# A linear-attention and SwiGLU kernel: w as token pairs, output weights four rows per partition, two sums moved from TensorE to VectorE, and another order

## The chip, the cores and the metric

The kernel runs on one core of one Trainium2 chip. The metric is the device time of one execution in microseconds (us). TensorE is called PE in the profile, its weight loads PEld, VectorE DVE, ScalarE ACT, GpSimd POOL and SyncE SP.

## What is computed

A linear attention with decay (batch 4, 8 heads, 768 tokens, 48 channels per head) feeds an RMS norm and a SwiGLU feed-forward layer (FFN) over 3072 tokens of width 384, with 1536 hidden units.

```python
for t in range(S):                                   # r, k, v, w: [4, 8, 768, 48]
    cur = einsum('bhd,bhe->bhde', u[None] * k[:, :, t], v[:, :, t])
    y[:, :, t] = einsum('bhd,bhde->bhe', r[:, :, t], state + cur)
    state = w[:, :, t, :, None] * state + einsum('bhd,bhe->bhde', k[:, :, t], v[:, :, t])
x = y.transpose(0, 2, 1, 3).reshape(3072, 384)
xn = x / sqrt(mean(x * x, -1) + 1e-6) * rms_g
g = xn @ w_gate
out = (g * sigmoid(g) * (xn @ w_val)) @ w_out
```

Inputs and the output are float32 in HBM; the matmuls take bf16.

## The kernel before, in words

The 768 tokens are cut into six superblocks n = 0 to 5 of 128 tokens; each has four batches j = 0 to 3. A block (n, j) is 128 tokens on the partitions by 8 heads x 48 channels. The recurrence inside a block becomes matmuls: with the sums of log w over the tokens, r and k are scaled by exponentials of these sums, their products are masked to the past, and a state per head carries what earlier blocks left. When the four blocks of a superblock are through, its 512 normalized tokens go through the FFN as 12 hidden groups f of 128 units.

Every piece of work is a small function of (n, j) or (n, f), and the string ORDER calls them one by one. The scheduling is by hand: each engine executes its instructions in just that order, and each DMA queue issues in it too. The steps that matter here, with their lines:

- load_w, load_k, load_r, load_v (L221, L208): 192 KB each, on SP's queue, 128 partitions x 8 heads x 192 bytes. Eight buffers of each kind; at most eight of SP's DMAs are under way, since each waits for the one eight places before it.
- ln (L195 through the helper act): the logarithm of w on ScalarE. cs_mm (L370, L373, L375): on TensorE the sums of log w before each token (mask_lt, into ps_a), the whole block's decay as four one-column products, and minus the sums from each token on (mask_nle, into ps_b).
- exp_r, exp_k (ScalarE), r_mul, k_mul (VectorE, L397, L402): the scaled r and k, as bf16 in rk. In superblock 1 the exponentials go to SBUF tiles er and ek.
- rk_pe and rk_tr: r and k transposed, in superblocks 0 and 1 by TensorE (L425) and a ScalarE copy (L434), later by DMA transposes on SP's queue (L430).
- q_mm (L443, L445), q_mask_e, q_copy_o, q_mask_o: the products of r and k, masked. y_mm (L488, L491): the block's output. st_mm (L468, L471) and st_new (L479): the new state, which is the old one (L468, a matmul with the identity) plus k times v, times the decay.
- bonus_mul (L408, L409), bonus_sum (L413), bonus_v (L418): the u term, mostly on GpSimd.
- x_add (L496), x_sq, x_rstd, xn_mul, then xn_pe and xn_out or, in superblocks 4 and 5, xn_tr (a DMA transpose) and xn_gain: the normalized tokens, transposed, as xnt.
- gate_mm and val_mm (L546), silu, h_mul (L564), o_mm (L606), o_out, out_dma: the FFN. ps_a and ps_b have two banks each, so gate_mm of group f waits for silu of f-2, and val_mm for h_mul of f-2.
- load_gv (L306) and load_wo (L312): the FFN's weights, on GpSimd's own queue, cast to bf16 on the way. load_gv.0 brings hidden groups 0 to 3, load_gv.1 groups 4 to 11; the last figure is 0 for the gate, 1 for the value. The first of each pair waits until load_w.1.0 has landed; load_wo waits for load_v.1.1. All stand among GpSimd's other steps and are issued in its turn.

Of the kernel before, what the change touches and what calls it, by code (L numbers as in the profile page):

```python
# [9 lines left out]
FP32 = mybir.dt.float32  # L10
BF16 = mybir.dt.bfloat16
AF = mybir.ActivationFunctionType
ALU = mybir.AluOpType

LN_EXP = "natural_log_exp_and_others"
# [10 lines left out]
load_w.0.0 load_v.0.0 load_w.0.1 load_k.0.0 load_r.0.0 ln.0.0 load_w.0.2 load_r.0.1 ln.0.1 cs_mm.0.0 load_k.0.1  # L26
cs_mm.0.1 exp_k.0.0 load_w.0.3 exp_r.0.0 k_mul.0.0 bonus_mul.0.0 exp_r.0.1 r_mul.0.0 load_r.0.2 exp_k.0.1 w_tot.0.0
cast_v.0.0 rk_pe.0.0 load_k.0.2 ln.0.2 r_mul.0.1 st_mm.0.0 rk_tr.0.0 cs_mm.0.2 load_w.1.0 st_new.0.0 bonus_mul.0.1
load_v.0.1 q_mm.0.0 k_mul.0.1 ln.0.3 w_tot.0.1 bonus_sum.0.0 rk_pe.0.1 load_k.0.3 exp_k.0.2 q_mask_e.0.0 exp_r.0.2
cs_mm.0.3 bonus_v.0.0 q_mask_o.0.0 rk_tr.0.1 load_r.0.3 k_mul.0.2 y_mm.0.0 bonus_mul.0.2 exp_k.0.3 load_w.1.1  # L30
r_mul.0.2 q_mm.0.1 exp_r.0.3 x_add.0.0 ln.1.0 rk_pe.0.2 load_v.0.2 bonus_sum.0.1 x_sq.0.0 q_mask_e.0.1 cast_v.0.1
load_v.0.3 bonus_v.0.1 w_tot.0.2 rk_tr.0.2 q_mask_o.0.1 cs_mm.1.0 load_w.1.2 k_mul.0.3 bonus_mul.0.3 q_mm.0.2
bonus_sum.0.2 load_k.1.0 r_mul.0.3 ln.1.1 q_mask_o.0.2 rk_pe.0.3 load_w.1.3 x_rstd.0.0 cast_v.0.2 y_mm.0.1 bonus_v.0.2
load_r.1.0 rk_tr.0.3 x_add.0.1 load_gv.0.0 load_r.1.1 q_mask_e.0.2 cast_v.0.3 xn_mul.0.0 load_gv.0.1 bonus_sum.0.3
q_mm.0.3 ln.1.2 bonus_v.0.3 y_mm.0.2 x_sq.0.1 q_mask_e.0.3 st_mm.0.1 exp_k.1.0 load_gv.1.1 w_tot.0.3 x_add.0.2
x_rstd.0.1 cs_mm.1.1 q_mask_o.0.3 exp_r.1.0 load_gv.1.0 x_sq.0.2 y_mm.0.3 exp_k.1.1 load_v.1.0 xn_pe.0.0 x_rstd.0.2
x_add.0.3 st_mm.0.2 st_new.0.1 xn_mul.0.1 x_sq.0.3 st_new.0.2 st_mm.0.3 cs_mm.1.2 x_rstd.0.3 xn_out.0.0 xn_mul.0.2
# [12 lines left out]
load_r.2.0 cs_mm.2.0 q_copy_o.1.3 h_mul.0.11 y_mm.1.2 x_sq.1.0 load_w.2.2 st_mm.1.2 x_add.1.1 o_mm.0.0 st_new.1.2  # L50
x_rstd.1.0 x_sq.1.1 load_r.2.1 exp_k.2.0 x_rstd.1.1 ln.2.1 load_k.2.1 k_mul.2.0 exp_r.2.0 q_mask_o.1.3 bonus_sum.1.3
o_mm.0.1 cast_v.1.3 load_r.2.2 o_out.0.0 xn_mul.1.0 bonus_v.1.3 w_tot.2.0 x_add.1.2 load_v.2.0 bonus_mul.2.0 x_sq.1.2
y_mm.1.3 load_v.2.1 o_out.0.1 st_mm.1.3 x_add.1.3 ln.2.2 cs_mm.2.1 load_w.2.3 st_new.1.3 o_mm.0.2 x_sq.1.3 x_rstd.1.2
exp_k.2.1 r_mul.2.0 load_k.2.2 xn_mul.1.1 x_rstd.1.3 k_mul.2.1 xn_mul.1.2 bonus_sum.2.0 out_dma.0.0 cs_mm.2.2
exp_r.2.1 cast_v.2.0 o_out.0.2 xn_pe.1.0 xn_pe.1.1 load_r.2.3 r_mul.2.1 bonus_mul.2.1 xn_pe.1.2 xn_mul.1.3 o_mm.0.3
xn_out.1.0 exp_r.2.2 load_k.2.3 xn_out.1.1 ln.2.3 rk_tr.2.0 xn_out.1.2 exp_k.2.2 w_tot.2.1 r_mul.2.2 cast_v.2.1
xn_pe.1.3 cs_mm.2.3 o_out.0.3 bonus_mul.2.2 xn_out.1.3 st_mm.2.0 load_v.2.2 exp_r.2.3 w_tot.2.2 st_mm.2.1 k_mul.2.2
load_k.3.0 exp_k.2.3 gate_mm.1.0 r_mul.2.3 w_tot.2.3 val_mm.1.0 load_r.3.0 silu.1.0 k_mul.2.3 bonus_mul.2.3
gate_mm.1.1 bonus_sum.2.1 rk_tr.2.1 val_mm.1.1 q_mm.2.0 silu.1.1 h_mul.1.0 gate_mm.1.2 load_r.3.1 bonus_v.2.0
h_mul.1.1 load_k.3.1 val_mm.1.2 silu.1.2 q_mask_e.2.0 gate_mm.1.3 h_mul.1.2 rk_tr.2.2 bonus_mul.3.0 val_mm.1.3  # L60
silu.1.3 st_new.2.0 gate_mm.1.4 q_copy_o.2.0 rk_tr.2.3 bonus_sum.2.2 val_mm.1.4 h_mul.1.3 silu.1.4 cast_v.2.2
# [596 lines left out]
```

## Time and profile before

| | us |
|---|---|
| median of 5 runs | 213.05 (212.78 to 213.16) |
| the profiled execution | 212.78 |
| its span (first to last instruction) | 210.8 |
| first FFN matmul starts | 29.67 |
| first o_mm starts | 56.27 |
| first FFN matmul of superblock 5 starts | 175.74 |
| last matmul ends | 207.54 |
| HBM read / written | 25.96 MB / 4.72 MB |

The profile's page gives each engine's busy time and share of the span, and a line of digits per engine: the span in 40 equal slices of 5.3 us, each digit the busy tenths of a slice (9 is 90% or more). Groups of instructions are named by line, engine, operation and tiles (output, an arrow, inputs). A timeline line reads: start, duration, engine, line, operation, tiles, shape, count, and in brackets the idle time before it and what ended that. A line of stretches reads: from:to, length, then for PE, PEld, DVE, ACT and POOL the busy time and the number of instructions, then TensorE's granted clock, the DMA engines' mean busy share and GB/s. A DMA queue's line reads: packets, MB, and the packets' time as a share of 16 engines. A matmul's own duration holds its latency, which overlaps the next; the spacing of starts is its price.

### The profile page before, as it was taken

The page shows a single profiled execution, that of the slowest core. Times are in us where ns is not written, and L with a number is a line of the kernel's source. Part 1 is how long each engine was busy: PE and PEld are TensorE (multiplying, and loading weights), DVE is VectorE, ACT ScalarE, POOL GpSimd, SP SyncE. Part 2 cuts the span into 40 slices and gives each one's busy share as a digit, 9 for nine tenths or more (in the row PEclk, how much of TensorE's full clock was granted, in tenths as well). Part 3 has the DMA queues.
Part 4 walks back from the last instruction along what each step waited for, and adds up shares of the span by engine and source line. Part 5 has one row for each costly group of instructions (what it writes and reads, how often), then busy time and mean ns, then how long its engine had stood idle before and what let it go on. Part 6 is the DMA issues. An engine that isn't in the chain of part 4 may idle for free.

```text
span 210.8 us, 4399 instructions
## 1 busy us (share of the span) xinstructions
PE 195.1 (93%) x1552; PEld 107.4 (51%) x1552; DVE 148.5 (70%) x295; ACT 138.4 (66%) x282; POOL 109.2 (52%) x167
## 2 busy tenths in 40 slices
PE   5676879799899999999999999999999999999993
PEld 2454533454566445665454665455655544544563
DVE  6498852899979778988689699767876755235411
ACT  3786995567988556987546998578858873225300
POOL 3498500698699593798697789573222520000000
PEclk9999999999999999999999999999999999999999
DMA  6999999999999999999999999981187030000122
GB/s 128 210 201 177 170 201 201 210 182 210 173 192 236 167 185 226 210 210 192 211 192 208 197 249 171 227 181 44 54 190 124 20 84 13 37 0 37 40 112 76
DMA packets 126878, 32.41 MB, mean 154 GB/s; under 512 B 120580, under 2 KB 126088, under 8 KB 126856
## 3 DMA queue, kind: packets, MB, share of 16 engines
q1 hardware_dynamic: 123664, 28.58, 67.3%
q0 software_dynamic: 3184, 3.54, 10.2%
q8 instruction: 12, 0.20, 0.4%
q14 instruction: 10, 0.08, 0.1%
q10 hardware_dynamic: 8, 0.00, 0.0%
HBM read 25.96 MB, written 4.72 MB: 146 GB/s over the span
## 4 chain that ended last, share of the span: by engine, by line
PE 72%; DMA 10%; SPq 9%; DVE 4%; issue 2%; ACT 1%; ACTq 0%
PE ps_q L606 22%; PE ps_a L546 19%; PE ps_b L546 19%; DMA rt<-in_r_dram 8%; SPq L208 6%; SPq L221 3%; PE ps_q L443 2%; DMA rkT<-rk 2%; PE ps_q L491 2%; PE ps_q L488 2%; PE ps_b L375 1%; DVE ht L564 1%; PE ps_a L370 1%; DVE rk L397 1%; PE ps_q L468 1%
## 5 line engine op out<-in xcount | busy, mean ns | idle before, releaser
L564 DVE TENSOR_TENSOR ht<-ps_b,sg 128x512 bf16<-128x512 f32 x72 | 48.6, 688 | 25.1 <-PE ps_b L546 17.6
L195 ACT ACTIVATE sg<-ps_a 128x512 bf16<-128x512 f32 x72 | 42.7, 596 | 35.0 <-PE ps_a L546 34.7
L546 PE MATMUL ps_b<-xnt,wv_sb 128*128 128x512 bf16 x216 | 59.1, 382 | 0.8 <-DVE ht L564 0.7
L546 PE MATMUL ps_a<-xnt,wg_sb 128*128 128x512 bf16 x216 | 59.7, 386 | 0.0
L606 PE MATMUL ps_q<-wo_sb,ht 128*128 128x384 bf16 (+1 forms) x300 | 49.9, 319 | 0.0
L408 POOL TENSOR_TENSOR ruk<-rt,kt 128x384 f32<-128x384 f32 x24 | 24.3, 1012 | 24.8 <-DMA rt<-in_r_dram 21.3
L606 PEld LDWEIGHTS <-ht 128*128 128x128 bf16 x300 | 28.4, 98 | 16.8
L546 PEld LDWEIGHTS <-wg_sb 128*128 128x128 bf16 x216 | 20.2, 99 | 23.3 <-issue 1.5
L546 PEld LDWEIGHTS <-wv_sb 128*128 128x128 bf16 x216 | 20.1, 98 | 23.2 <-issue 2.7
L409 POOL TENSOR_TENSOR ruk<-ruk,u_bc 128x384 f32<-128x384 f32 x24 | 24.6, 1023 | 1.9
L418 POOL TENSOR_TENSOR ydiag<-vt,diag 128x384 f32<-128x384 f32 x24 | 19.8, 831 | 3.1 <-DVE diag L413 2.9
L461 POOL TENSOR_SCALAR_AFFINE_SELECT qts<-qts 128x512 bf16<-128x512 bf16 x20 | 12.7, 637 | 14.3 <-ACT qts L454 14.3
L450 DVE TENSOR_TENSOR qts<-ps_q,mask_lt 128x512 bf16<-128x512 f32 x24 | 16.2, 684 | 4.0 <-issue 2.5
L496 DVE TENSOR_TENSOR xb<-ps_q,ydiag 128x384 f32<-128x384 f32 x24 | 13.2, 552 | 5.3 <-PE ps_q L491 4.8
L195 ACT ACTIVATE lw<-wt 128x384 bf16<-128x384 f32 x24 | 12.0, 515 | 5.2 <-DMA wt<-in_w_dram 5.1
L501 ACT ACTIVATE junk<-xb 128x384 bf16<-128x384 f32 x24 | 12.4, 518 | 3.9 <-DVE xb L496 3.8
L514 ACT ACTIVATE xn<-xb,rstd 128x384 bf16<-128x384 f32 x24 | 14.4, 606 | 0.9 <-POOL rstd L510 0.6
L454 ACT CAST qts<-ps_q 128x512 bf16<-128x512 f32 x20 | 11.6, 584 | 4.7 <-PE ps_q L445 4.7
L193 ACT ACT_TABLE_LOAD x10 | 12.8, 1283 | 1.8 <-PEq L642 1.6
L613 DVE COPY ob<-ps_q 128x384 f32<-128x384 f32 (+1 forms) x13 | 7.0, 538 | 9.1 <-PE ps_q L606 9.0
L615 ACT COPY ob<-ps_q 128x384 f32<-128x384 f32 (+1 forms) x12 | 5.6, 463 | 11.9 <-PE ps_q L606 11.9
L402 DVE TENSOR_TENSOR rk<-kt,ps_b 128x384 bf16<-128x384 f32 x20 | 11.0, 548 | 3.3 <-DMA kt<-in_k_dram 1.6
(71 smaller groups left out, 276.4 us busy)
## 6 DMA issues: line engine op xcount, KB each, us to landing
wt<-in_w_dram SPq DMA_DIRECT2D x24, 192.0 KB, 4.0
vt<-in_v_dram SPq DMA_DIRECT2D x24, 192.0 KB, 4.1
kt<-in_k_dram SPq DMA_DIRECT2D x24, 192.0 KB, 3.8
rt<-in_r_dram SPq DMA_DIRECT2D x24, 192.0 KB, 3.8
out_dram<-ob SPq DMA_DIRECT2D x23, 192.0 KB, 2.8
wo_sb<-in_moe_w_out_dram POOLq DMA_DIRECT2D x3, 384.0 KB, 7.4
wv_sb<-in_moe_w_val_dram POOLq DMA_DIRECT2D x1, 768.0 KB, 10.9
wg_sb<-in_moe_w_gate_dram POOLq DMA_DIRECT2D x1, 768.0 KB, 14.4
```

What stands on the lines that cost most here:

```text
L193: nc.scalar.preload_act_table_set(table_name)
L195: return nc.scalar.activation(**kw).ins
L408: nc.gpsimd.tensor_tensor(out=ruk[n, j], in0=inp["r", n, j], in1=inp["k", n, j], op=ALU.mult)
L409: nc.gpsimd.tensor_tensor(out=ruk[n, j], in0=ruk[n, j], in1=u_bc, op=ALU.mult)
L418: nc.gpsimd.tensor_tensor(out=ydiag[n, j], in0=inp["v", n, j], in1=diag[n, j].to_broadcast([128, H, D]), op=ALU.mult)
L450: nc.vector.tensor_tensor(out=qts[n, j][:, 0], in0=bank["q", n, j][0], in1=bc_mid(mask_lt, NP), op=ALU.mult)
L461: nc.gpsimd.affine_select(out=qts[n, j][:, 1], in_=qts[n, j][:, 1], compare_op=ALU.is_gt, fill=0.0, base=0, pattern=[[0, NP], [1, 128]], c ...
L496: nc.vector.tensor_tensor(out=xb[n, j], in0=bank.pop(("y", n, j)), in1=ydiag[n, j].rearrange("p h d -> p (h d)"), op=ALU.add)
L514: nc.scalar.activation(out=xn, in_=xb[n, j], func=AF.Copy, scale=rstd[n, j][:, 1:2])
L546: nc.tensor.matmul(ps, lhsT=ws[:, c, f * 128:(f + 1) * 128], rhs=xnt[n][:, c, :], start=(c == 0), stop=(c == KC - 1))
L564: nc.vector.tensor_tensor(out=ht[n][:, f, :], in0=bank.pop(("v", n, f)), in1=bank.pop(("sg", n, f)), op=ALU.mult)
L606: nc.tensor.matmul(ps[:, cols], lhsT=ht[n][:, f, b * L:(b + 1) * L], rhs=wo_sb[:, f, cols], start=(f == 0), stop=(f == FC - 1))
```

## The change

- W_PAIR = (0, 1): w of superblocks 0 and 1 is loaded with two neighbouring tokens per partition (384 bytes in a row), batch j even on partitions 0 to 63 and j odd on 64 to 127. One ln and one cs_mm then serve two batches; cs_pair makes the sums with 64-row matmuls (eight of 384 columns and sixteen of one column for two batches) and masks mp_lt and mp_nle, which GpSimd builds at the start, after its other constants.
- load_wo puts four consecutive rows of w_out on one partition. So hidden unit 4m + i of a group of 512 stands at partition m, and the gate and value weights are read with a step of four columns (units).
- The gate and value weights have one tile for each load (wg_sb0, wg_sb4, wv_sb0, wv_sb4).
- OLD_DVE = (2, 3, 4): the old state is added by VectorE in PSUM, not by a matmul with the identity.
- ONE_SUM = (4, 5): the sum for k is made by VectorE from the sum for r and log w (cs_add); exp_k takes it with a factor of -1, and the mask_nle matmul goes.
- ORDER is replaced by another.

```diff
-    W_PAIR = ()
+    W_PAIR = (0, 1)
     Q_PAIR = ()
-    OLD_DVE = ()
+    OLD_DVE = (2, 3, 4)
+    ONE_SUM = (4, 5)
...
-    wg_sb = persist.tile([128, KC, DF], BF16)
-    wv_sb = persist.tile([128, KC, DF], BF16)
+    wg_sb = [persist.tile([128, KC, (b - a) * 128], BF16, name="wg_sb%d" % a) for a, b in zip(GV, GV[1:])]
+    wv_sb = [persist.tile([128, KC, (b - a) * 128], BF16, name="wv_sb%d" % a) for a, b in zip(GV, GV[1:])]
...
-            in_=moe_w_out[g * FG * 128:(g + 1) * FG * 128, :].rearrange("(c p) m -> p c m", p=128)).ins
+            in_=moe_w_out[g * FG * 128:(g + 1) * FG * 128, :].rearrange("(p c) m -> p c m", c=FG)).ins
...
-        nc.tensor.matmul(b[:, 0:DM].rearrange("p (h d) -> p h d", h=H), lhsT=mask_nle, rhs=rhs,
-                         start=True, stop=True)
+        if n not in ONE_SUM:
+            nc.tensor.matmul(b[:, 0:DM].rearrange("p (h d) -> p h d", h=H), lhsT=mask_nle, rhs=rhs,
+                             start=True, stop=True)
+
+    def cs_add(n, j):
+        b = bank["cs_k", n, j] = psB.tile([128, 512], FP32, name="ps_b")
+        nc.vector.tensor_tensor(out=b[:, 0:DM].rearrange("p (h d) -> p h d", h=H),
+                                in0=bank["cs_r", n, j][:, NP:NP + DM].rearrange("p (h d) -> p h d", h=H),
+                                in1=lw[:, n % 2, j, :, 0:D], op=ALU.add)
...
+    def units(ws, c, f):
+        g = max(i for i, x in enumerate(GV) if x <= f)
+        a = (f // FG * FG - GV[g]) * 128
+        return ws[g][:, c, a:a + FG * 128].rearrange("p (m i) -> p i m", i=FG)[:, f % FG, :]
+
     def fc_mm(ps, ws, n, f):
         for c in range(KC):
-            nc.tensor.matmul(ps, lhsT=ws[:, c, f * 128:(f + 1) * 128], rhs=xnt[n][:, c, :],
+            nc.tensor.matmul(ps, lhsT=units(ws, c, f), rhs=xnt[n][:, c, :],
```

The add of the old state was in the code already, behind the switch: st_new begins with `nc.vector.tensor_tensor(out=ps, in0=ps, in1=st[:, n % 2, j], op=ALU.add)` for a superblock in OLD_DVE, and st_mm leaves its identity matmul out.

The new order up to the first FFN groups, in the parts that the prediction speaks of. SP's queue:

```text
before: w00 v00 w01 k00 r00 w02 r01 k01 w03 r02 k02 w10 v01 k03 r03 w11 v02 v03 w12 k10 w13 r10 r11 v10 k11 v11 k12 k13 r12 r13 w20 v12 ...
after:  w00 w01 k00 r00 k01 v00 r01 k02 w02 r02 w03 v01 v02 w10 r03 k03 w11 r10 k10 w12 w13 k11 r11 v03 k12 r12 v10 v11 k13 r13 v12 w20 ...
```

GpSimd's queue, from bonus_mul.0.3 on:

```text
before: bonus_mul.0.3 bonus_v.0.2 load_gv.0.0 load_gv.0.1 bonus_v.0.3 load_gv.1.1 load_gv.1.0 bonus_mul.1.0 ...
after:  bonus_mul.0.3 bonus_mul.1.0 bonus_v.0.2 load_gv.0.0 load_gv.0.1 bonus_v.0.3 load_gv.1.0 bonus_mul.1.1 load_gv.1.1 ...
```

TensorE, from xn_pe.0.2 on (cs_mm.1.3 stood here before; after, all sums of superblock 1 are done):

```text
before: xn_pe.0.2 xn_pe.0.3 cs_mm.1.3 gate_mm.0.0 val_mm.0.0 gate_mm.0.1 val_mm.0.1 gate_mm.0.2 val_mm.0.2 gate_mm.0.3 val_mm.0.3 rk_pe.1.0 gate_mm.0.4 val_mm.0.4 ...
after:  rk_pe.1.0 xn_pe.0.2 xn_pe.0.3 gate_mm.0.0 val_mm.0.0 gate_mm.0.1 rk_pe.1.1 q_mm.1.0 val_mm.0.1 gate_mm.0.2 val_mm.0.2 q_mm.1.1 gate_mm.0.3 val_mm.0.3 rk_pe.1.2 st_mm.0.1 gate_mm.0.4 val_mm.0.4 ...
```

In the rest, attention and FFN stay interleaved as before, with single steps moved by a few places. st_mm.0.1, 0.2 and 0.3 come after the first FFN groups instead of before them.

## The prediction

> **What bounds the kernel now.** I read the page's busy table first, then its slices.
>
> ```profile
> PE 195.1 (93%) x1552; PEld 107.4 (51%) x1552; DVE 148.5 (70%) x295; ACT 138.4 (66%) x282; POOL 109.2 (52%) x167
> ...
> PE   5676879799899999999999999999999999999993
> ...
> DMA  6999999999999999999999999981187030000122
> ```
>
> TensorE is full from the seventh slice on; before that it has holes, while the DMA engines are full from the second slice to the 27th. So there are two regimes. I cut the span where they meet: the first FFN matmul (29.67 us), the end of the last long wait (38.06), the first output matmul (56.27), the first FFN matmul of superblock 5 (175.74). The busy times of these stretches, in the order PE, weight loads, DVE, ACT, POOL:
>
> ```profile
> 0.00:29.67 29.67, 19.93 (x177) 12.49 (x177) 21.27 (x48) 21.99 (x51) 16.30 (x28) 1.00 0.98 180
> 29.67:38.06 8.39, 7.11 (x25) 2.68 (x24) 2.63 (x7) 4.54 (x7) 0.49 (x1) 1.00 1.14 209
> 38.06:56.27 18.21, 17.40 (x169) 9.52 (x170) 17.89 (x29) 13.87 (x22) 14.86 (x17) 1.00 1.14 200
> 56.27:175.74 119.47, 119.04 (x1007) 65.53 (x1005) 94.26 (x195) 89.08 (x187) 77.51 (x122) 1.00 0.84 168
> ```
>
> Up to 38 us the DMA sets the pace; from 38 to 56 VectorE has 17.89 of 18.21 us filled and TensorE waits for it here and there; from 56 on TensorE is never free and VectorE has 94.26/119.47 = 79%. What ends the first regime is one load, seen in the timelines of VectorE and TensorE:
>
> ```profile
> 37.44 0.56 DVE L397 TENSOR_TENSOR rk<-rt,er 128x384 bf16<-128x384 f32 x1 [2.45 <-DMA rt<-in_r_dram]
> ...
> 38.06 0.62 PE L425 MATMUL ps_q<-ident,rk 128*128 128x128 bf16 x8 [1.28 <-DVE rk L397]
> ```
>
> In the chain of waits this load (load_r.1.0) lies from 20.97 to 37.42 us, 16.4 us for a transfer that takes 3.8 at the median. The DMA view of 23 to 36 us says why:
>
> ```profile
> q0 software_dynamic: 1458, 2.18, 91.8%
> q1 hardware_dynamic: 2107, 0.40, 23.9%
> ```
>
> Weights (POOL's queue, q0) and loads (SP's, q1) share the engines roughly packet against packet. A weight packet takes 96 or 172 ns and a load's 192-byte packet 15 ns (the trace's packet records), so while weights flow SP's queue nearly stands: 2107 packets, two loads, in 13 us, against one load in 0.95 us before (17,358 packets of 1024 per load from 4 to 20 us). The weight phase ran from its first packet at 21.8 us to its last at 37.1 us, 15.3 us.
>
> **The price list of TensorE** is the spacing of starts where nothing waits:
>
> ```profile
> 55.14 0.32 PE L370 MATMUL ps_a<-lw,mask_lt 128*128 128x384 bf16 x1
> 55.31 0.24 PE L373 MATMUL ps_a<-ones_col,lw 128*128 128x1 bf16 x4
> 55.41 0.32 PE L375 MATMUL ps_b<-lw,mask_nle 128*128 128x384 bf16 x1
> 55.57 0.33 PE L488 MATMUL ps_q<-st,rkT 128*128 128x96 bf16 x4
> 55.74 0.36 PE L491 MATMUL ps_q<-vb,qts 128*128 128x48 bf16 x8
> 55.94 0.32 PE L468 MATMUL ps_q<-st,ident 128*128 128x384 bf16 x1
> 56.10 0.33 PE L471 MATMUL ps_q<-vb,rk 128*128 128x96 bf16 x4
> ```
>
> A 384-column matmul costs 0.16 us, cs_mm 0.43, y_mm 0.37, st_mm 0.33 (half of it the old state); in the same way gate_mm or val_mm is 0.65, o_mm 1.95, rk_pe 0.46, q_mm 0.33. Summed over the order, the program needs 179.3 us of TensorE.
>
> **Token pairs and the new load order.** Eight loads of w have 512 packets of 384 bytes in place of 1024 of 192. Packets of 192, 256 and 768 bytes took 15, 18 and 36 ns, so 384 bytes lies between 18 and 36, near 22 by the straight line; a load then takes 512 x 22.5 ns / 16 engines = 0.72 us in place of 0.96. But each fills only 64 partitions, which no row shows, so I keep 0 to 0.24 us saved per load (a loss is possible too, if fewer engines share it; loads queued behind would fill the others). The Trainium skill, "SBUF — State Buffer", section "Door 1: The DMA port swizzle", speaks against it: a transfer to partitions 0 to 63 reaches half of the ports and ran at 196 GB/s there. By that a pair load is 1.0 us, nothing is saved, and my sum would be about 1 us higher.
>
> SP's queue now takes r and k of batches 0 and 1 and k of batch 2 of superblock 1 ahead of the weights, and v.0.3 only as its 24th load (18th before). POOL issues the first weights after bonus_mul.1.0, which needs k.1.0, the 19th load. The first load landed at 3.76 us and the next followed 0.96 apart, so the 19th lands at 3.76 + 18 x 0.96 = 21.0, less six pair loads, 19.6 to 21.0. POOL adds bonus_mul (2.07) and bonus_v (0.83): the first weights are issued at 22.6 to 24.0 in place of 19.91, the first packet follows 1.9 later as it did before, the phase takes 14.3 to 15.3, and landing 0.5 more: **the last gate/val weights are there at 39.3 to 41.7 us, not 37.64**. I take 40.6, in the middle. The attention of superblock 0 ends near 30 us as now: v.0.3 lands at 23.9 to 25.8, and bonus_v, x_add, x_sq, x_rstd, xn_mul, xn_pe, xn_out follow with 5 us (0.83, 0.56, 0.61, 0.52, 0.60, 0.50, 0.56 and hand-overs). So val_mm.0.4, which reads the last piece, starts at 40.6 instead of 39.16: **+1.4 us** (0.1 to 2.5). Queued behind it on TensorE is the whole FFN, and behind that VectorE's h_mul.
>
> The paired cs_mm (24 matmuls for two batches, 12 before) comes wholly before the first FFN matmul. Eight 384-column products on half the rows cost 0.65 us if the two halves run side by side, 1.3 if not; q_mm's eight 128-column products on 48 rows take 0.33 us where 8 x 0.053 = 0.43 would be serial, so halves do overlap, and I take 1.05 with the 16 one-column ones. TensorE is busy 19.93 of 29.67 us there, which hides 4 x 0.2 us. The extra masks on POOL (ten instructions near 0.3 us, as its mask rows) end near 5.8 us, when the first pair of w is through its Ln: at most 0.5 us, before a start that the loads set anyway.
>
> **What TensorE has left at val_mm.0.4.** By the order: 163.9 us before, 159.4 after. The 4.5 us are: twelve old-state matmuls gone, 12 x 0.1625 = 1.95; eight mask_nle matmuls gone, 1.30; rk_pe.1.1, 1.2 and q_mm.1.0, 1.1 already done while weights were awaited, 1.58; st_mm.0.2 and 0.3 still to do, +0.34.
>
> **Stalls after it.** Before, 39.16 to 207.54 is 168.4 us for 163.9 of work: 2.1 stalled until o_mm.0.0, 2.4 after it. Until o_mm.0.0 VectorE's work falls from 16.4 to 11.9 us (r_mul and k_mul of three batches, 0.56 to 1.26 us each, are done earlier) against 13.6 of TensorE; I take 0.7, a gain of 1.4. Afterwards VectorE gets twelve adds of the old state and eight of the decay sum; x_add, which reads PSUM and SBUF likewise, takes 552 ns, so 11.0 us more, 105 of about 116: 90% instead of 79%. TensorE lost about 2 us in the 18 us where VectorE had 98%, and 2.4 in the 151 after; I take 1.5 more, nearer to the latter.
>
> **The weights' layout.** Output weights come as 128 larger packets per load instead of 512; at the straight line through 79, 96 and 172 ns for 768, 1024 and 2048 bytes a 3072-byte packet takes 250 ns, 2.0 us per load instead of 2.5, hidden at 45 to 57 us behind the FFN. They also hold SP's queue harder (24 turns per engine instead of 96); the loads behind are due at 49 us or later, and if v.1.2 misses that, it costs 1 to 2 us. Gate and val weights are now read with a step of four elements. No row has such a read: below 216 ns per weight load it costs nothing, since 0.648 us per three matmuls covers the present 98 ns; a load of 300 ns would cost 432 x 0.084 = 36 us. I take nothing, the nearest row being 98. The skill's "TensorE: Matmul & The Clock Gate", section "Weight-path perf modes — Fast Weight Load (FWL) and DoubleRow", lets the fast load take such a step, and its section "LDWEIGHTS (loading the stationary operand)" gives P/1.2, 107 ns for 128 columns, without it; only its remark on 16-byte lines in "SBUF — State Buffer" speaks of a penalty. By either the sum stays.
>
> **The sum**, against the profiled execution (212.78 us, span 210.8; the median of the runs is 213.05): +1.4 - 4.5 - 1.4 + 1.5 = -3.0, so **209.8 us**.
>
> **Rivals.** (1) *VectorE becomes the bound*, from o_mm.1 to the FFN of superblock 4. Against it: 25.2 us of VectorE lie free there and only 11 are asked for. For it: from o_mm.2.0 to gate_mm.3.0 the new order has 10.3 us of VectorE for 9.8 of TensorE, and the add stands in st_new ahead of the scaling while h_mul waits behind it, which frees the PSUM that val_mm needs. If each of three such stretches loses 2 us, as 38 to 56 did, with 1.5 already counted: 209.8 + 4.5 = 214.3, slower. It decides once the added stalls exceed 4.5 us. (2) *The weights come later still*: v.0.3 or v.1.0, now last in SP's queue, are caught behind weight packets (48 turns per engine at 187 ns); cast_v.1.0 then holds ScalarE's silu.0.5. 1 to 3 us: 211 to 212.8. (3) *The strided weight read is not hidden*: 213 to 245. (4) *The new order's stalls vanish altogether* and pairs save in full: 209.8 - 1.5 - 1.2 = 207.1.
>
> **Numbers.** Forecast with (4) 0.48, all but 0.02 of it faster; rival (2) 0.19, of it 0.12 faster, 0.04 the same, 0.03 slower; rival (1) 0.28, slower but for 0.02 faster; (3) 0.05, slower. Faster by over 0.2% (what a measurement here can tell from no change): 0.60; the same 0.06; slower 0.34. The range 206.8 to 215.2 leaves out the strided case, the worst of (1) and some luck below; the forecast's own is 207.0 to 212.0.
>
> **What would show it.** Right: wv_sb's last piece landing near 40.6, rk_pe.1.0 ahead of the first gate_mm, no wait of 1 us on r of superblock 1, TensorE's busy time down by some 2.5 us, VectorE's up to about 158, gate_mm spacing still 0.65. Wrong: waits of val_mm on h_mul between 85 and 160 us; loads of v landing beyond 45 us with silu waiting; gate_mm spacing above 0.65; paired loads as slow as plain ones.

## The result, and the profile after

The changed kernel takes 214.23 us (median of 43 runs, 213.05 to 216.54) against 213.01 us (80 runs) for the kernel before: a ratio of 1.0068 [1.0054, 1.0081], 0.7% slower where 209.8 us was forecast. Some executions of every kernel fall into a slower state; all ratios here compare executions in the faster one, while the medians of the experiments take in all of theirs. Its profiled execution took 214.61 us, span 212.9.

The busy table and two slice lines of the page after, as they were shown of before:

```profile
PE 193.6 (91%) x1580; PEld 114.5 (54%) x1580; DVE 158.2 (74%) x315; ACT 137.7 (65%) x278; POOL 112.5 (53%) x177
...
PE   3367775999999999999999899999999999999993
...
DMA  5999999999997999887999869994398031100022
```

TensorE is busy 1.5 us less (2.5 forecast) and VectorE 9.7 us more (158 forecast). But TensorE's slices are thinner at the start (3 3 6 7 against 5 6 7 6), and it is full only from the eighth slice on. The same stretches, cut at the first gate_mm, val_mm.0.4, the first o_mm and the first FFN matmul of superblock 5 (from:to, length, then PE, weight loads, DVE, ACT, POOL):

```profile
0.00:35.10 35.10, 20.18 (x221) 13.96 (x221) 23.64 (x47) 22.25 (x48) 24.04 (x42) 1.00 1.02 187
35.10:45.52 10.42, 10.42 (x63) 5.25 (x64) 4.95 (x8) 6.93 (x11) 3.88 (x5) 1.00 1.04 194
45.52:59.19 13.67, 13.50 (x118) 7.67 (x117) 12.53 (x25) 10.39 (x20) 8.33 (x13) 1.00 1.04 200
59.19:178.33 119.14, 118.14 (x1005) 69.33 (x1003) 105.47 (x219) 89.08 (x186) 76.27 (x119) 1.00 0.81 164
```

The start is 35.10 us long instead of 29.67. Behind it TensorE is never free again: val_mm.0.4 does not wait for weights, and VectorE, with 105.47 of 119.14 us (89%, forecast 90%), holds up nothing for long. From val_mm.0.4 to the last matmul (209.66) it is 164.14 us; before it was 168.38 (39.16 to 207.54). So the forecast's -4.4 for everything behind val_mm.0.4 is measured as -4.24, and the whole error lies ahead of it: val_mm.0.4 starts at 45.52 instead of 39.16, **+6.4 where +1.4 was forecast**.

In one point these rows mislead. They give a granted clock of 1.00 from the start, but the traces of the two kernels hold no clock record ahead of 33.29 us (before) and 40.52 us (after). The matmuls show a slower TensorE until then. In the changed kernel a gate_mm or val_mm takes 1.28 us (36.33 to 37.61) until about 40.4 us, and 0.65 (44.88 to 45.52) behind that; before, the change comes at 33.4 us. The last line is val_mm.0.4, which starts without a wait:

```profile
36.33 1.48 PE L561 MATMUL ps_b<-xnt,wv_sb 128*128 128x512 bf16 x3
37.61 1.48 PE L561 MATMUL ps_a<-xnt,wg_sb 128*128 128x512 bf16 x3
...
44.88 0.81 PE L561 MATMUL ps_a<-xnt,wg_sb 128*128 128x512 bf16 x3
45.52 0.81 PE L561 MATMUL ps_b<-xnt,wv_sb 128*128 128x512 bf16 x3
```

The wait for load_r.1.0, which ended the start before, is gone. In its place TensorE waits for the normalization (timeline of TensorE, changed kernel; L435 is rk_pe.1.0, L535 xn_pe, L561 the first gate_mm):

```profile
31.08 1.06 PE L435 MATMUL ps_q<-ident,rk 128*128 128x128 bf16 x8
...
33.86 0.50 PE L535 MATMUL ps_q<-ident,xn 128*128 128x128 bf16 x3 [1.39 <-ACT xn L524]
35.10 1.44 PE L561 MATMUL ps_a<-xnt,wg_sb 128*128 128x512 bf16 x3 [0.74 <-DVE xnt L546]
```

xn comes from ScalarE, so the start is read on ScalarE. Its busy time up to the first silu, first of the kernel before, then of the changed one (ACT is the fourth pair of figures):

```profile
0.00:32.03 32.03, 22.29 (x182) 13.35 (x183) 21.90 (x49) 24.15 (x54) 16.30 (x28) 1.00 0.99 181
```

```profile
0.00:37.56 37.56, 22.64 (x226) 14.81 (x227) 23.64 (x47) 24.68 (x52) 24.04 (x42) 1.00 1.03 188
```

The work is the same, 24.15 and 24.68 us; the idle time is 7.9 us before and 12.9 after. Its waits for loads up to there (total, times, longest), of before, then of the changed kernel:

```profile
ACT lw L195 <- DMA wt<-in_w_dram: 5.1, 6, 1.4
ACT vb L330 <- DMA vt<-in_v_dram: 0.6, 1, 0.6
```

```profile
ACT lw L197 <- DMA wt<-in_w_dram: 6.8, 4, 2.2
ACT vb L332 <- DMA vt<-in_v_dram: 2.9, 1, 2.9
```

In the changed kernel these are 2.2 us for the first pair of w, 2.9 for v.0.0 (cast_v.0.0 stands ahead of exp_k.0.0), 1.2, 1.5 and 1.9 for w.0.3, w.1.1 and w.1.3. The last of these, in the timeline of ScalarE:

```profile
24.42 0.84 ACT L197 ACTIVATE lw<-wt 128x768 bf16<-128x768 f32 x1 [1.91 <-DMA wt<-in_w_dram]
25.17 0.51 ACT L511 ACTIVATE junk<-xb 128x384 bf16<-128x384 f32 x1
...
31.98 0.52 ACT L511 ACTIVATE junk<-xb 128x384 bf16<-128x384 f32 x1 [0.21 <-DVE xb L506]
...
37.56 0.60 ACT L197 ACTIVATE sg<-ps_a 128x512 bf16<-128x512 f32 x1
```

ln.1.2 waits for w.1.3, and the first x_sq of superblock 0 (L511) stands behind it. From there ScalarE has 13.1 us of queue, in which the timeline shows one gap, of 0.21 us, and the first silu is its end. Before, the last wait of this kind was cast_v.0.3:

```profile
21.06 0.51 ACT L330 CAST vb<-vt 128x384 bf16<-128x384 f32 x1 [0.63 <-DMA vt<-in_v_dram]
...
29.84 0.49 ACT L195 ACTIVATE ek<-ps_b 128x384 f32<-128x384 f32 x1 [0.23 <-PE ps_b L375]
...
32.03 0.60 ACT L195 ACTIVATE sg<-ps_a 128x512 bf16<-128x512 f32 x1
```

That is 10.97 us from the wait to the silu.

### The profile page after: what moved, and what is told of

Its sections match the earlier page's. It is cut to its first block, busy times and chain, and to the rows that moved or that the text cites. A ratio compares the mean times of both kernels' runs of the same rounds, so it can differ in the third digit from the quotient of the medians.

```text
span 212.9 us, 4495 instructions
## 1 busy us (share of the span) xinstructions
PE 193.6 (91%) x1580; PEld 114.5 (54%) x1580; DVE 158.2 (74%) x315; ACT 137.7 (65%) x278; POOL 112.5 (53%) x177
## 4 chain that ended last, share of the span: by engine, by line
PE 73%; DVE 8%; SPq 7%; ACT 3%; issue 3%; DMA 2%; POOL 2%; POOLq 0%; DVEq 0%; ACTq 0%
PE ps_q L621 21%; PE ps_a L561 20%; PE ps_b L561 20%; SPq L210 4%; SPq L223 3%; DMA kt<-in_k_dram 2%; PE ps_q L453 2%; DVE ht L579 2%; PE ps_q L501 1%; PE ps_q L498 1%; DVE rk L407 1%; PE ps_q L481 1%; PE ps_a L373 1%; PE ps_q L535 1%; ACT junk L511 1%
## 5 line engine op out<-in xcount | busy, mean ns | idle before, releaser
L561 PE MATMUL ps_a<-xnt,wg_sb 128*128 128x512 bf16 x216 | 59.9, 387 | 1.0 <-DVE xnt L546 1.0
L579 DVE TENSOR_TENSOR ht<-ps_b,sg 128x512 bf16<-128x512 f32 x72 | 49.2, 687 | 14.5 <-PE ps_b L561 10.1
L561 PE MATMUL ps_b<-xnt,wv_sb 128*128 128x512 bf16 x216 | 59.3, 384 | 0.1
L561 PEld LDWEIGHTS <-wg_sb 128*128 128x128 bf16 x216 | 23.4, 115 | 21.9 <-issue 2.9
L561 PEld LDWEIGHTS <-wv_sb 128*128 128x128 bf16 x216 | 22.9, 114 | 19.3 <-issue 1.5
L471 POOL TENSOR_SCALAR_AFFINE_SELECT qts<-qts 128x512 bf16<-128x512 bf16 x20 | 13.1, 656 | 20.8 <-ACT qts L464 20.8
L423 DVE TENSOR_REDUCE diag<-ruk 128x8 f32<-128x384 f32 x24 | 12.9, 544 | 5.2 <-POOL ruk L419 5.2
L628 DVE COPY ob<-ps_q 128x384 f32<-128x384 f32 (+1 forms) x13 | 7.0, 541 | 13.1 <-PE ps_q L621 13.0
L197 ACT ACTIVATE lw<-wt 128x384 bf16<-128x384 f32 (+1 forms) x20 | 11.3, 579 | 6.8 <-DMA wt<-in_w_dram 6.8
L519 POOL TENSOR_SCALAR rstd<-rstd 128x1 f32<-128x1 f32 x20 | 3.8, 192 | 19.3 <-ACT junk L511 18.9
L511 ACT ACTIVATE junk<-xb 128x384 bf16<-128x384 f32 x24 | 12.4, 518 | 2.3 <-DVE xb L506 2.3
L630 ACT COPY ob<-ps_q 128x384 f32<-128x384 f32 (+1 forms) x12 | 5.6, 464 | 12.9 <-PE ps_q L621 12.9
```

The lines of the kernel that those rows point to most:

```text
L197: return nc.scalar.activation(**kw).ins
L471: nc.gpsimd.affine_select(out=qts[n, j][:, 1], in_=qts[n, j][:, 1], compare_op=ALU.is_gt, fill=0.0, base=0, pattern=[[0, NP], [1, 128]], c ...
L511: nc.scalar.activation(out=junk, in_=xb[n, j], func=AF.Square, accum_out=rstd[n, j][:, 0:1])
L561: nc.tensor.matmul(ps, lhsT=units(ws, c, f), rhs=xnt[n][:, c, :], start=(c == 0), stop=(c == KC - 1))
L579: nc.vector.tensor_tensor(out=ht[n][:, f, :], in0=bank.pop(("v", n, f)), in1=bank.pop(("sg", n, f)), op=ALU.mult)
```

## The experiments

Two theories to begin with. **Theory "pairs"**: w as token pairs makes the start late, since logs and sums come two batches at a time. **Theory "order"**: the new order does it, with or without pairs. Later the second was split into the order of the loads and the order of the engines' steps. The table has the profiled executions' milestones (start of the step, us), and the median and the ratio to before; "sums" are the old state (OLD_DVE) and the decay sum (ONE_SUM) on VectorE.

| kernel | first gate_mm | val_mm.0.4 | first o_mm | gate_mm.1.0 | last matmul ends | median | ratio |
|---|---|---|---|---|---|---|---|
| before | 29.67 | 39.16 | 56.27 | 67.39 | 207.54 | 213.01 | 1 |
| after | 35.10 | 45.52 | 59.19 | 70.82 | 209.66 | 214.23 | 1.0068 [1.0054, 1.0081] |
| e1 | 35.19 | 44.49 | 58.41 | 70.05 | 208.87 | 214.42 | 1.0059 [1.0028, 1.0090] |
| e2 | 33.05 | 41.21 | 58.16 | 69.28 | 208.45 | 213.82 | 1.0046 [1.0016, 1.0076] |
| e4 | 29.23 | 38.02 | 54.42 | 65.44 | 211.62 | 216.06 | 1.0151 [1.0096, 1.0205] |
| e5 | 34.22 | 44.09 | 58.98 | 70.61 | 209.81 | 213.89 | 1.0059 [1.0031, 1.0088] |
| e6 | 34.75 | 44.12 | 59.20 | 70.83 | 210.09 | 214.49 | 1.0076 [1.0044, 1.0107] |
| e7 | 38.48 | 49.04 | 62.57 | 74.20 | 213.35 | 217.80 | 1.0214 [1.0167, 1.0262] |
| e9 | 29.18 | 38.24 | 54.65 | 65.87 | 207.94 | 212.77 | 0.9989 [0.9955, 1.0023] |
| e10 | 29.84 | 38.05 | 54.54 | 65.45 | 209.25 | 214.38 | 1.0063 [1.0025, 1.0101] |
| e11 | 33.57 | 42.13 | 60.26 | 71.90 | 210.86 | 216.17 | 1.0151 [1.0100, 1.0202] |
| e12 | 33.04 | 41.17 | 59.52 | 71.15 | 210.40 | 217.34 | 1.0198 [1.0139, 1.0258] |
| e13 | 30.28 | 38.36 | 54.70 | 67.98 | 207.08 | 212.08 | 0.9971 [0.9937, 1.0005] |
| e14 | 29.85 | 39.20 | 55.43 | 66.53 | 207.06 | 211.87 | 0.9936 [0.9900, 0.9972] |
| e16 | 34.85 | 45.19 | 58.93 | 70.56 | 212.34 | 216.56 | 1.0155 [1.0107, 1.0202] |

**e1: after without pairs.** `W_PAIR = ()`, each ln and cs_mm twice at its place.

> The changed kernel with its own order and all of its other parts, but with w of superblocks 0 and 1 loaded and summed block by block again (each paired ln and cs_mm becomes the two single ones, at the same place). Theory P, the pairs make the late start (two loads behind each logarithm, a sum on TensorE that is twice as long at the slow pace of the start, masks built first): the first FFN matmul falls from 35.1 to 32 us or less, and the time from 214.2 to 211 or less. Theory O, the new order makes it (its loads, and ScalarE's steps behind ln.1.2): 35 us and 214 remain.

The first gate_mm stays at 35.19 us and the time at 214.42. Theory "pairs" falls for this order: without them the start is as late. What ends it differs. Without pairs k.1.0, the 19th load in both, lands at 20.54 us instead of 22.15, so the weights are issued at 23.48 instead of 25.09 us and catch v.0.3, which lands at 30.00 (26.92 in the changed kernel). The timeline of ScalarE in e1:

```profile
30.03 0.51 ACT L332 CAST vb<-vt 128x384 bf16<-128x384 f32 x1 [0.82 <-DMA vt<-in_v_dram]
```

**e2: before with pairs.** `W_PAIR = (0, 1)` in the order of before; cs_mm.1.0, w_tot.0.3 and exp_r.1.1 moved by a few places, as the paired sums need.

> The kernel before with the pairs of w alone, in its own order; the odd ln and cs_mm fall away, and cs_mm.1.0, w_tot.0.3 and exp_r.1.1 are moved a few places, since a paired sum takes both banks at once. Theory P: the first FFN matmul moves from 29.7 to 33 us or more and the time to 216 or more. Theory O: 29 to 30.5 us and 212.5 to 213.5.

Pairs alone make this start 3.4 us later, and 0.9 of it is left at the last matmul (208.45 against 207.54). They are no help in either order, and as loads they are slower: k.1.0, the 20th load here, lands at 23.23 us instead of 22.48.

**e4: before's order with all the rest of the change.** Layout, both sums on VectorE (cs_add right behind cs_mm), plain loads of w. **e9: of that, the layout alone. e10: layout and OLD_DVE.**

```diff
-ORDER = (the new order)
+ORDER = (the order of before; in e4 with cs_add.4.j and cs_add.5.j behind cs_mm)
-    W_PAIR = (0, 1)
+    W_PAIR = ()
```

e9 also has `OLD_DVE = ()` and `ONE_SUM = ()`, e10 `ONE_SUM = ()`.

> The order of the kernel before, without pairs, but with everything else of the change: output weights four rows per partition, strided gate and value weights, the old state of superblocks 2 to 4 and the decay sum of 4 and 5 on VectorE (each cs_add right behind its cs_mm). If the prediction's sizes hold, TensorE has 1.95 + 1.30 us less and VectorE's 11 us more find room: 209.5 to 211, first FFN matmul at 29.7. If the adds on VectorE only pay in the new order (rival: VectorE becomes the bound): 213 or more, with val_mm waiting for h_mul after 85 us.

> The kernel before with only the new layout of the weights: four rows of the output weights per partition, gate and value weights read with a step of four columns, one tile per weight load. The prediction's step (hidden, costs nothing): 212.6 to 213.4 us, spacing of gate_mm's three matmuls 0.65 us, weight loads 115 instead of 98 ns. Rival: the 3072-byte packets hold SP's queue, so k.2.3 lands late as it did with the VectorE adds in this order, val_mm.1.1 stalls 1 to 2 us and the time is 214 or more.

> The order of before, the new layout, and of the two VectorE sums only the old state of superblocks 2 to 4. By the prediction's price this saves 12 x 0.16 = 1.95 us of TensorE's work and costs 0.9 of stalls, its share of the 1.5: 211.5 to 212.3 us. By the theory that the adds don't pay in an order which isn't made for them (both sums together in this order, with two more changes, gave 216.06), TensorE waits for VectorE behind st_new by more than it saves: 213.5 to 215.5. The difference to 216.06 is then the decay sum's.

The layout costs nothing over the run (e9, 0.9989). It even brings the first o_mm 1.6 us forward, which is lost again when k.2.3 comes late. VectorE's and TensorE's lines of e9:

```profile
69.01 0.56 DVE L411 TENSOR_TENSOR rk<-kt,ps_b 128x384 bf16<-128x384 f32 x1 [1.56 <-DMA kt<-in_k_dram]
```

```profile
69.62 0.81 PE L560 MATMUL ps_b<-xnt,wv_sb 128*128 128x512 bf16 x3 [1.27 <-DVE rk L411]
```

The old state on VectorE makes that order slower, 214.38 against 212.77 us, though by the prediction's price TensorE has 1.95 us less to do. With the decay sum as well (e4) it is 216.06; e4 and e9 differ in the two sums alone, by 1.6% in their ratios. The sums of TensorE's waits (total, times, longest) between the first o_mm and the FFN of superblock 5, first of before, then of e10, then of the changed kernel:

```profile
PE ps_q L443 <- DMA rkT<-rk: 0.4, 1, 0.4
```

```profile
PE ps_b L560 <- DVE ht L578: 2.1, 4, 0.9
PE ps_b L560 <- DVE rk L411: 1.6, 1, 1.6
PE ps_a L372 <- DVE rk L406: 0.5, 1, 0.5
PE ps_a L560 <- DVE wcol L403: 0.5, 1, 0.5
```

```profile
PE ps_a L373 <- ACT lw L197: 0.4, 1, 0.4
PE ps_a L561 <- DVE xnt L546: 0.2, 1, 0.2
```

e10 has 4.7 us of waits where before has 0.4. Not all of them come from the old state: e9, with the layout alone, has 1.9 us there, 1.3 of them the wait for k.2.3 (1.6 in e10). But val_mm waits for h_mul 0.2 us in e9 and 2.1 in e10, as the prediction's rival (1), VectorE as the bound, describes it. So that rival's mechanism is real in before's order. The new order has 0.6 us of waits in all.

**e16: after with both sums back on TensorE** (`OLD_DVE = ()`, `ONE_SUM = ()`, no cs_add).

> The changed kernel with both sums back on TensorE: no VectorE add of the old state, no VectorE add for the decay sum (cs_add is left out, the mask_nle matmul stands in cs_mm). TensorE gets 3.25 us of work more, VectorE 11 us less. The prediction's price (3.25 of work saved for 1.5 of stalls): 1.7 us slower than the changed kernel, 215.6 to 216.4 us. If VectorE's stalls take it all, no slower than the changed kernel: 213.5 to 214.5.

```profile
58.93:181.01 122.08, 120.12 (x1014) 71.27 (x1023) 96.41 (x199) 88.97 (x186) 76.03 (x119) 1.00 0.81 163
```

This stretch is 122.08 us instead of 119.14, and the run 216.56 instead of 214.23 us; as a difference of the two ratios 0.87% (0.4 to 1.4% by their intervals), 1.9 us. The prediction's price was 1.7. In the new order, then, the sums on VectorE are a gain, and near the forecast one.

**e5, e6, e7, e11: repairs of the start, pairs kept.** e5 puts ln.1.2 behind xn_mul.0.0 and cs_mm.1.2 behind y_mm.0.3. e6 adds: load_v.0.3 ahead of load_r.1.0, cast_v.0.0 behind exp_k.0.1, bonus_sum.0.0 behind r_mul.0.0. e7 adds: weights ahead of bonus_mul.1.0. e11 adds: r_mul, k_mul and rk_pe of superblock 1 behind the first FFN groups, bonus_mul.1.0 and 1.1 behind all weights. **e12** is e11 with plain loads.

> The changed kernel with two steps moved: ln.1.2 (which waits for w.1.3) behind x_sq.0.0, x_rstd.0.0 and xn_mul.0.0 on ScalarE, and cs_mm.1.2 behind y_mm.0.3 on TensorE. Theory S, the start is late because ScalarE waits in its queue for the pair's second load with the norm of superblock 0 behind it, and y_mm.0.3 stands behind a paired sum that waits for a bank: the first FFN matmul falls to 33 us or less, the time by as much, to 212.5 or less. Rival, the loads themselves are late (v.0.3, the weights): 34.5 to 35.5 us, 213.8 to 214.5.

> The changed kernel with five steps of its start moved, token pairs and all else kept: cast_v.0.0 behind exp_k.0.1 on ScalarE, bonus_sum.0.0 (with bonus_v.0.0) behind r_mul.0.0, load_v.0.3 ahead of load_r.1.0, ln.1.2 behind xn_mul.0.0, cs_mm.1.2 behind y_mm.0.3. Theory O (the places of single steps in the new order make the start late, not the token pairs): exp_k.0.0 starts near 6.5 us instead of 9.30, v.0.3 is no longer awaited, and the first gate_mm starts at 31 to 32.5 us instead of 35.10. The weights are issued no earlier (25 us), so val_mm.0.4 still waits for the last piece at 43.5 to 44.5; time 212.6 to 213.6. Theory P (token pairs make it late: their sums and logs come two batches at a time): the first gate_mm stays at 34 us or later, time 213.9 as with two of these moves alone.

> As the run before it, and the first FFN weights are issued ahead of bonus_mul.1.0 on GpSimd instead of behind it. Theory O: they are then issued near 22 to 23 us instead of 25, the last gate and val weights land near 40.5, val_mm.0.4 starts at 41 to 42 instead of 45.52, and nearly all of that reaches the end: 210.8 to 212.0 us. Rival W (weights that come earlier only hold up the loads of superblock 1 more, packet against packet): k and r of superblock 1 land later, rk_pe.1.0 or q_mm.1.0 stalls ahead of the first FFN groups, and the time stays at 212.6 or more.

> The changed kernel (token pairs and all else kept) with the repaired start of two runs before, the first weights ahead of bonus_mul.1.0, and in addition the work of superblock 1 taken out of the start again: r_mul and k_mul of its batches 0 and 1, bonus_sum.1.0 and rk_pe.1.0 and 1.1 stand behind the first FFN groups, bonus_mul.1.0 and 1.1 behind all four weight loads. Theory S (the first FFN matmul is late because VectorE, ScalarE and GpSimd have work of superblock 1 queued ahead of superblock 0's norm and of the weights, and this work needs five more loads): no wait on r or k of superblock 1 before the first gate_mm, which starts at 31 to 33 us (35.10 in the changed kernel, 38.48 with the weights first); all weights are issued by 28 us and landed by 40.5, val_mm.0.4 starts at 40 to 42; the time is 211 to 213 us, since 1.6 us of TensorE's work that filled the wait stands behind it again. Rival P (token pairs alone make it late): first gate_mm at 34 or later. Rival L (the DMA engines are full, and what the start gains the loads of superblock 1 lose later): first gate_mm early, but waits on r or k of superblock 1 in the FFN groups of superblock 0, time 213.5 or more.

> The same order with plain loads of w, one logarithm and one set of sums per batch. Theory S with the pairs' own price of 0.5 to 1 us: first gate_mm at 30 to 31.5 us, time 210.3 to 212.2. If pairs are worth their fewer packets it is no faster than with them.

These are mostly misses. e5 gives 0.9 us at the first gate_mm and nothing significant in time. e6 has v.0.3 at 21.32 and exp_k.0.0 early, as wanted, but w.1.1 now lands later (ScalarE waits 2.6 us until 20.97), and 15.6 us of ScalarE's queue to the first silu begin there: 34.75. In e7 the earlier weights hold k.1.1, and k_mul.1.1 waits for it (4.8 us, until 34.1) on VectorE ahead of x_add.0.3: 38.48. e11 has val_mm.0.4 at 42.13, 3.4 us earlier than the changed kernel, and yet its first o_mm at 60.26, since r.1.2 lands at 41.55, rk_pe.1.2 waits 1.4 us for VectorE at 48.00, and TensorE's 1.6 us of attention stand behind the weights again. Each repair met the next late load. e12, without pairs, has its first gate_mm at 33.04 us and takes 217.34 us, outside the 30 to 31.5 and 210.3 to 212.2 expected. Two runs are inconclusive: e8 (e7 with plain loads), 215.11 us, spread from 212.20 to 217.34, and e15 (before's order up to the second FFN, the new one behind it), 214.04 us, from 210.09 to 214.51; nothing is read from them.

> As the run before it, with plain loads of w and one logarithm and one set of sums per batch, at the same places. If the token pairs cost something by themselves (they made the first gate_mm of the kernel before 3.4 us later, and the whole 0.8 us slower), this is 0.5 to 1.5 us faster than the same order with pairs: 209.5 to 211.0. If the pairs are worth their 17 percent fewer packets, it is as much slower: 211.5 to 213.

> The order of before up to the second FFN (gate_mm.1.0), the new order behind it, plain loads of w, the rest of the change kept. gate_mm.1.0 near 65.5 to 67 us, as with the old state alone or the layout alone in the order of before. If the new order behind it runs in its 138.8 us (71 to 210 in the changed kernel): last matmul at 204.5 to 206, 208 to 210 us. Rival: k.2.3 lands near 67 us in this order, val_mm.1.0 or 1.1 stalls 1.5 to 2 us, last matmul at 206.5 to 207.5, 210.5 to 211.5.

**e20, e21, e22: the order of the loads by itself.** Engines' steps as before, layout as after, plain loads of w, sums on TensorE; all transposes by TensorE, so only these three are compared in time. e21 changes one thing, the order of SP's first 31 loads; e22 also puts bonus_mul.1.0 ahead of the weights, as the changed kernel has it.

> Base for the two runs behind it: the order of before with the new layout of the weights, plain loads of w, both sums on TensorE, and the transposes of superblocks 2 to 5 (r and k, the normalized tokens of 4 and 5) made by TensorE with a copy on ScalarE or VectorE, as in superblocks 0 and 1, so that no DMA transposes. Up to the first o_mm nothing else changes: first gate_mm near 29.2 us, o_mm.0.0 near 54.6, as with the layout alone. Behind it TensorE has 16 x 0.46 + 8 x 0.2 = 9 us more, 221 us or more; only its start and the differences to it are read.

> The base with one thing of the new order: the order in which SP issues its first 31 loads. All steps of the engines, the weights' issue on GpSimd too, stay in the order of before. The weights are issued near 21 us, ahead of v.0.3's place (24th load, due at 3.76 + 23 x 0.96 = 25.8), so v.0.3 is caught behind weight packets. Theory L (the order of the loads makes the start late): first gate_mm at 34 us or later. Theory Q (the engines' steps of superblock 1 ahead of the norm make it late): 29.5 to 31.5.

> As the run before it, and bonus_mul.1.0 stands ahead of bonus_v.0.2 and of the weights on GpSimd, as in the changed kernel, so the weights come some 3 us later and v.0.3 ahead of them, near 26 us. Theory Q, and the prediction's own step (v.0.3 at 23.9 to 25.8, then 5 us): first gate_mm at 30.5 to 32 us, last weight landing near 40 to 41.5, o_mm.0.0 near 57. Theory L: first gate_mm at 34 us or later, o_mm.0.0 at 58.5 or later.

| | v.0.3 lands | cast_v.0.3 starts | first gate_mm | first silu | median | ratio to before |
|---|---|---|---|---|---|---|
| e20 | 21.17 | 21.20 | 29.86 | 32.23 | 225.97 | 1.0629 [1.0597, 1.0662] |
| e21 | 30.33 | 30.35 | 38.96 | 41.33 | 235.49 | 1.1067 [1.1022, 1.1112] |
| e22 | 25.57 | 25.59 | 34.19 | 36.56 | 231.13 | 1.0884 [1.0837, 1.0930] |

The loads' order alone is enough for a late start: +9.1 us with the weights in their old place, where they catch v.0.3 (e21). With bonus_mul.1.0 moved too, so that the weights come late as in the changed kernel, it is +4.3 (e22). (e9, which has the same start as e20, starts its first gate_mm at 29.18 us, so neither step is smaller against it.) Here the prediction's step is tried in its own terms. In e22 v.0.3 lands at 25.57 us, in the forecast's 23.9 to 25.8, and the first gate_mm follows not 5 but 8.6 us later. The timeline of ScalarE in e22:

```profile
25.59 0.51 ACT L333 CAST vb<-vt 128x384 bf16<-128x384 f32 x1 [4.37 <-DMA vt<-in_v_dram]
26.01 0.61 ACT L523 ACTIVATE xn<-xb,rstd 128x384 bf16<-128x384 f32 x1
...
36.56 0.60 ACT L198 ACTIVATE sg<-ps_a 128x512 bf16<-128x512 f32 x1
```

Behind cast_v.0.3 stands the normalization of all four batches and superblock 1's logs and exponentials. From this wait to the first silu it is 10.97 us, the same as in before (10.97) and within 0.06 of e20 and e21 (11.03, 10.98). In e1, where cast_v.0.3 comes late in the queue, it is 5.2 us from v.0.3 to the first gate_mm, near the forecast's 5.

**e13: the order of before up to the first o_mm, the new order behind it**, plain loads, layout and sums as after. **e14**: also bonus_mul.2.0 behind x_rstd.1.2 and bonus_mul.2.1 behind x_rstd.1.3 on GpSimd.

> The order of the kernel before up to the first o_mm, the new order from there on, plain loads of w, and the rest of the change: layout, old state and decay sum on VectorE. Theory S: the start of before gives o_mm.0.0 at 54.4 to 56.3 us (59.19 in the changed kernel), and from there the new order needs its 150.5 us to the last matmul: 204.9 to 206.8 in place of 207.54, time 210.2 to 212.2, faster than both. Rival L (loads that have to come in any order set the pace until some 70 us, so a start that is 3 to 5 us earlier only meets them earlier, as k.2.3 did in the order of before with these adds): waits on k or r of superblock 2, gate_mm.1.0 at 68 us or later, time 213 or more.

> As the kernel with the start of before and the new order behind it, but bonus_mul.2.0 stands behind x_rstd.1.2 and bonus_mul.2.1 behind x_rstd.1.3 on GpSimd, bonus_sum.2.0 beside bonus_sum.2.1 on VectorE. If the wait of the normalization for GpSimd behind r.2.0 is what cost the 1.7 us between o_mm.0.0 and the second FFN: gate_mm.1.0 at 66.0 to 66.6 us instead of 67.98, 210.4 to 211.0 us, faster than before. If TensorE is held there by the exponentials or the loads of superblock 2 as well: gate_mm.1.0 at 67.5 or later, 212 us.

e13 has the start back: first gate_mm at 30.28 us and first o_mm at 54.70. It differs from e1 in the order up to the first o_mm alone (neither has pairs), and that turns 35.19 us into 30.28 and a ratio of 1.0059 into 0.9971. It gives 1.7 us of this away before the second FFN: r.2.0 lands at 57.63, bonus_mul.2.0 waits for it, and x_rstd behind it on GpSimd holds ScalarE's xn_mul.1.1, the exponentials behind that, and TensorE's cs_mm.2.2. The three timelines of e13 (GpSimd, ScalarE, TensorE):

```profile
57.77 1.00 POOL L418 TENSOR_TENSOR ruk<-rt,kt 128x384 f32<-128x384 f32 x1 [1.31 <-DMA rt<-in_r_dram]
```

```profile
61.58 0.61 ACT L524 ACTIVATE xn<-xb,rstd 128x384 bf16<-128x384 f32 x1 [1.64 <-POOL rstd L520]
```

```profile
63.66 0.34 PE L373 MATMUL ps_a<-lw,mask_lt 128*128 128x384 bf16 x1 [1.55 <-DVE wcol L404]
```

e14 takes that out: gate_mm.1.0 at 66.53, as expected. Its time, 211.87 us, misses the 210.4 to 211.0 expected. One wait stands out, st_mm.2.0's for cast_v.2.0, which stands behind the moved bonus_mul on GpSimd; that it makes up the miss is not shown:

```profile
68.29 0.33 PE L481 MATMUL ps_q<-vb,rk 128*128 128x96 bf16 x4 [0.95 <-POOL vb L334]
```

Still e14 is faster than both kernels: 0.9936 [0.9900, 0.9972] of before.

## Why the prediction was wrong, step by step

- **The start, the step that failed.** It said: "The attention of superblock 0 ends near 30 us as now: v.0.3 lands at 23.9 to 25.8, and bonus_v, x_add, x_sq, x_rstd, xn_mul, xn_pe, xn_out follow with 5 us". Both halves were off: v.0.3 landed at 26.92 us, and the first gate_mm came 8.2 us later. The 5 us are the chain of one batch. But ScalarE takes its steps in the order given and has next to no gap there: what follows its last wait for a load is its whole queue, 10.97 us to the first silu in before (a figure that the trace of before already held) and 13.14 in the changed kernel. In e22 v.0.3 landed within the forecast and the start was late all the same, so the second half fails by itself. e21 shows the load order alone to be enough; e5 and e6 show that moving the steps around ln.1.2 and v.0.3 is not enough to undo it; e13 against e1 shows that the start of before is. How the 2.8 us between e12 (33.04) and e13 (30.28) divide among single loads and steps stays open.
- **The weights at 40.6 us: late as well, but not the last thing waited for.** They landed at 43.24, beyond the 39.3 to 41.7: k.1.0 landed at 22.15 (19.6 to 21.0 forecast; 20.54 without pairs, in e1), the first weights were issued at 25.09, and the last of the four only at 31.01, behind bonus_mul.1.1. By themselves they would have put val_mm.0.4 at 43.24, an estimated 4.1 us later than before. It came at 45.52, because TensorE was busy all the way from the late first gate_mm. In e5, whose first gate_mm is 0.9 us earlier, it does wait for the weights, at 44.09.
- **The price list, taken at 55 us, does not hold at the start.** At its figures the work from the first gate_mm up to val_mm.0.4 (five gate_mm, four val_mm, two rk_pe, two q_mm and st_mm.0.1 at half price) is 7.6 us; it took 10.42, as the matmuls ran at half that pace until 40.4 us. By this estimate val_mm.0.4 would have been ready near 42.7 us at the listed pace, and the weights would have held it.
- **TensorE's work and stalls behind val_mm.0.4: right in sum**, -4.24 us for -4.4, with some luck. Until the first o_mm the stretch is 3.44 us shorter than before (forecast 2.8: 1.4 of work, 1.4 of stalls), behind it 0.80 (forecast 1.6), and the two misses cancel. Until the first o_mm TensorE is free for 0.2 of 13.67 us (VectorE has 12.53 filled, where it had 98% before), and VectorE's 11 us of adds cost little in an order made for them (e16), more in the old one (e10, e4). The rival that VectorE becomes the bound did not come about, but its mechanism is shown by e10.
- **Pairs: they save nothing and cost something, and in before's order the cost is not hidden** (e2). The 16th load landed at 18.76 us, not before 3.76 + 15 x 0.96 = 18.16; with plain loads in the same order it landed at 17.66 (e1). By the 19th load the pairs are 1.6 us behind (22.15 and 20.54; in e16 and e22 alike, 22.06 and 20.58), where 0 to 1.4 us saved was forecast. The GB/s line has 208 and 206 in slices 2 and 3 against 210 and 201 before. The Trainium skill, "SBUF — State Buffer", section "Door 1: The DMA port swizzle", has it that a transfer to partitions 0 to 63 reaches half of the ports; that nothing is saved in these rows agrees with it. The paired sums took 1.7 us for two batches (22.46 to 24.14) where 1.05 was forecast. The masks on GpSimd ended at 6.64 us (5.8 forecast); cs_mm.0.0 waited 0.21 us for them and 1.54 for its pair of logs.
- **The layout: right.** The weight groups of the page after:

```profile
L621 PEld LDWEIGHTS <-ht 128*128 128x128 bf16 x300 | 28.2, 98 | 16.5
L561 PEld LDWEIGHTS <-wg_sb 128*128 128x128 bf16 x216 | 23.4, 115 | 21.9 <-issue 2.9
L561 PEld LDWEIGHTS <-wv_sb 128*128 128x128 bf16 x216 | 22.9, 114 | 19.3 <-issue 1.5
```

  The read with a step of four takes 115 ns instead of 99, below the 216 at which it would show; gate_mm keeps its 0.65 us. The 3072-byte packets took 247 ns (250 estimated).
- **The sum.** 212.78 + 6.36 (start) - 4.24 (behind it) - 0.29 (around the last matmul and the span) = 214.61. Of the 4.8 us by which the forecast missed it, 4.96 come from the start; the rest nearly cancels.

## What to carry to other kernels

When an order is changed at a start that is bound by loads, take for each in-order engine the last wait for a load in its queue and add the whole queue behind it: that, not the chain of one item, is when the next stage can begin. A load that moves back by six places costs its six load times there even if it is "only" needed by the last batch, and work for the next stage put ahead of it fills waits only if its own loads don't come first. Price moved sums by running them both ways in the order that is meant for them: the same two sums cost 1.6% in one order (e4 against e9) and won 0.9% in the other (after against e16). And look at the matmuls' own spacing before a price list is used at a start: here it was half the later pace until 33 us in one kernel and 40 us in the other.

## What the runs showed of the hardware

- While weights flow, loads nearly stand. In the changed kernel from 27 to 43 us (DMA view: packets, MB, share of 16 engines), 4.3 loads in 16 us:

```profile
q0 software_dynamic: 1600, 2.36, 83.3%
q1 hardware_dynamic: 4422, 0.84, 32.5%
```

- TensorE ran its matmuls at half pace at the start and once more behind a wait. In both kernels the first gate_mm takes 1.23 us instead of 0.65. Where a trace holds a clock record, half pace and a granted clock of 0.50 stand together: in e4 val_mm waits 1.78 us until 69.76 us, and from 71.16 to 74.57 us gate_mm and val_mm take 1.28 us each (the clock is the last figure but two):

```profile
71.16:74.57 3.41, 3.41 (x10) 1.24 (x9) 1.95 (x4) 0.60 (x1) 2.44 (x4) 0.50 1.13 218
74.57:80.00 5.43, 5.43 (x33) 2.73 (x31) 4.99 (x11) 2.69 (x5) 4.23 (x6) 1.00 1.05 201
```

  In e9 the granted clock is 0.50 from 15.60 to 32.67 us and 1.00 behind that. What sets it was not tried.
- One r_mul (r_mul.1.0, 128 x 384) took 1.92 us at 28.29 where others take 0.55; only once, and not explained.
